# Beginning the moves of a tile's left-over rows from SyncE instead of GpSimd

## The chip, the cores and the metric

The kernel runs on one NeuronCore of a Trainium2 chip. The metric is the device time of one launch in microseconds (us), the median of several runs. Three runs of the kernel before gave 1610.87, 1610.90 and 1611.31 us; the median is 1610.9 us.

## The reference, cut to what matters

Four blocks follow each other over one sequence of 2048 tokens of 512 features: A, B, A, B. Each adds its result to x.

```
x = x + A(layernorm(x));  x = x + B(layernorm(x));  x = x + A(...);  x = x + B(...)

A:  mem = mem0                                # 8 rows
    for s in range(64):                       # 64 segments of 32 tokens, one after the other
        h = concat([mem, xs])                 # 8 + 32 rows
        q, k, v = h@Wq, h@Wk, h@Wv            # 32 heads of 128
        o = softmax(mask(q k^T * scale)) v;  o = o @ Wo
        mem = o[:8];  outs.append(o[8:])      # the memory feeds the next segment

B:  linear attention: kv = sum phi(k) v over all tokens; o = phi(q) kv / (phi(q) z); o @ wo
```

Block A is a recurrence: the first 8 rows of a segment's output are the memory of the next one. Block B needs a sum over all tokens before any of its outputs.

## The kernel before, in words

**Tiles and steps.** The 2048 tokens are 16 tiles of 128 rows. A tile holds four segments, so block A walks through 64 steps s, and tile G = s // 4, g = s % 4. The weights Wq, Wk, Wv and Wo stay in SBUF. Per step TensorE (PE) projects the step's block, forms the scores, multiplies probabilities with v, and projects with Wo (`out_proj`, L1388). VectorE (DVE) and ScalarE (ACT) empty PSUM, and make the softmax.

**Left-over rows.** A step's matmul block has room for 32 rows: 8 of memory and 24 of the segment's 32. The last 8 rows of each of the four segments of a tile ("left") are collected in one block of 32 rows per tile, computed once (`left_block`, L1181), and projected once per tile (`left_rows`, L1445). So rows come back in two ways: 24 rows per step, and 4 times 8 rows per tile.

**Bringing rows home.** `rows_out` (L1434) adds two halves of the projection on DVE (L1437) into a small staging tile `y_sb[:, k]`, and then moves rows by DMA from SBUF to SBUF into `dx_sb`, at the partitions where they belong. k is 0 for a step's 24 rows (two moves of 24x256 elements, 12 KB each), and 1 for the left rows (eight moves of 8x256, 4 KB each; six for the last tile). At the end of a tile one DVE addition (`residual`, L1476) adds `dx_sb` to the tile's x; it waits for all moves of the tile, by the semaphore counts `dy0` and `dy1`. The layer norm of block B (L1099) follows on DVE.

**Who begins the DMAs.** All moves go through `x_move` (L954 and L955), whose default engine is GpSimd (POOL). POOL's queue also holds the stores of x and of the queries to DRAM, the loads of tiles, and in `load_wo_b` (L983) the load of block B's output weight into `MB_sb` (512 KB, a part of the arena), once for each of the two B blocks. SyncE (SP) loads the weights at the start, then begins nothing until the end of the last A block, where `last_rows` (L1625) reloads queries and x with eight loads (L1636), and the results are stored (L1683).

**The order of the work.** It is written out: each operation has a planned time in a table (`PERIOD`, `OWN`), all are sorted by it, and each engine gets its operations in that order. An engine runs its list strictly in order, and each operation waits for the semaphores of what it depends on. So an operation that waits holds back all behind it on its engine. PSUM banks are given out along the same order. The planned times do not depend on the engine that begins a DMA.

On POOL the second weight load stands in the list just ahead of the eight left moves of the tile before the last, and these ahead of two moves of a step's rows. SP's list has, in the kernel before, the loads at the start and then at once the loads of `last_rows`.

Of the kernel before, what the change touches and what calls it, by code (L numbers as in the profile page):

```python
# [596 lines left out]
def c_dve(n, rate=1):  # L597
    return 0.155 + 1.044e-3 * n / rate
# [32 lines left out]
class _Prog:  # L631
# [19 lines left out]
    def add(self, engs, fn, cost, reads=(), writes=(), tiles=(), dsem=None, after=(), lat=0.0, quad=(0, 0), mode=0):  # L651
        nd = _Node()
        nd.lat = lat
        nd.quad = quad
        nd.mode = mode
        nd.key = self.place + (self.count,)
        self.count += 1
        nd.engs = (engs,) if isinstance(engs, str) else tuple(engs)
        nd.cost = cost if isinstance(cost, dict) else {e: cost for e in nd.engs}
        nd.fn = fn  # L660
        nd.sync = set(after)
        nd.order = {self.before[e] for e in nd.engs if e in self.before}
        nd.tiles = tuple(tiles)
        nd.dsem = dsem
        nd.eng = nd.know = None
        nd.sig = False
        nd.val = 0
        nd.waits = []
        nd.idx = len(self.nodes)
        if dsem is not None:  # L670
            self.dma_tot[dsem] = self.dma_tot.get(dsem, 0) + 16
            nd.dval = self.dma_tot[dsem]
        for key in reads:
            st = self.res.setdefault(key, [None, []])
            if st[0] is not None:
                nd.sync.add(st[0])
            st[1].append(nd)
        for key in writes:
            st = self.res.setdefault(key, [None, []])
            if st[0] is not None and st[0] is not nd:  # L680
                nd.sync.add(st[0])
            for r in st[1]:
                if r is not nd:
                    nd.sync.add(r)
            st[0] = nd
            st[1] = []
        for tl in nd.tiles:

            pe = [o for o in tl.ops if o.engs == ("pe",)]
            if nd.engs == ("pe",):  # L690
                if pe:
                    nd.order.add(pe[-1])
                nd.sync.update(tl.ops[tl.ops.index(pe[-1]) + 1:] if pe else [])
            else:
                nd.sync.add(pe[-1])
            tl.ops.append(nd)
        self.nodes.append(nd)
        return nd
# [122 lines left out]
def _build_kernel(nc, A_x, A_mem0, A_Wq, A_Wk, A_Wv, A_Wo, A_seg_len, B_wqkv, B_wo, out):  # L821
# [132 lines left out]
    def x_move(o, i, k, reads, writes, kind, eng="pool", lat=2.0):  # L954
        add(eng, lambda e: e.dma_start(o, i), 0.55 if eng == "pool" else 0.4, reads=reads, writes=writes,  # L955
            dsem="%s%d" % (kind, k), lat=lat + (0.4 if eng == "pool" else 0.0))
# [63 lines left out]
    for j in range(4):  # L1020
        q = slice(32 * j, 32 * j + 32)
        d = j % 2
# [107 lines left out]
    def a_layer(layer):  # L1130
# [303 lines left out]
        def rows_out(w, tl, G, moves):  # L1434

            k = int(w == NW - 1)
            add("dve", lambda v: v.tensor_tensor(y_sb[0:64, k, :], tl.f32()[0:64, 0:256], outW[64:128, w, :].bitcast(F32),  # L1437
                                                 ALU.add),
                c_dve(256), reads=[("outW", w, 0), ("outW", w, 1)], tiles=[tl], writes=[("y", k)], quad=(2, 0))
            for i, (src, dst, n) in enumerate(moves):  # L1440
                for d in range(2):
                    x_move(dx_sb[dst:dst + n, G % 2, 256 * d:256 * d + 256], y_sb[32 * d + src:32 * d + src + n, k, :], k,
                           [("y", k)], [("dx", G % 2, dst, d)], "dy")

        def left_rows(G):  # L1445
            w, tl = out_proj(oTl[:, G % 2, :, :], [[("oTl", G % 2, b)] for b in range(2)], False)
            rows_out(w, tl, G, [(8 * g, 32 * g + 24, 8) for g in range(4 if G < NT - 1 else 3)])

        def residual(G, g, w):

            at(4 * G + g + 1, "res")
            w, tl = w
            xk = ("x", slot(G))
            x = x_sb[:, slot(G), :]
            if G == NT - 1 and g == 3:
                tz = P.tile()

                def pick(pe):
                    for d in range(2):
                        r = pe.matmul(tz.f32()[:, 256 * d:256 * d + 256], selz_sb[:, d, :], outW[:, w, :], start=d == 0,  # L1460
                                      stop=d == 1, skip_group_check=True)
                    return r
                add("pe", pick, 0.42, reads=[("outW", w, 0), ("outW", w, 1), "selz"], tiles=[tz], mode=1)
                add("dve", lambda v: v.tensor_tensor(x, x, tz.f32()[:, :], ALU.add), c_dve(512),
                    reads=[xk], writes=[xk], tiles=[tz])
                return
            rows_out(w, tl, G, [(8, 32 * g, 24)])
            if g == (3 if G < NT - 1 else 2):
                n = 128
                if G < NT - 1:  # L1470
                    left_rows(G)
                else:
                    n = 96
                    at(NSEG - 1, "lr")
                    left_rows(G)
                add("dve", lambda v: v.tensor_tensor(x[0:n, :], x[0:n, :], dx_sb[0:n, G % 2, :], ALU.add), c_dve(512, 2),  # L1476
                    reads=[xk] + [("dx", G % 2, 32 * i + r, d) for i in range(n // 32) for r in (0, 24) for d in range(2)],
                    writes=[xk])
# [26 lines left out]
        for s in range(NSEG):  # L1505
            G, g = divmod(s, 4)
# [233 lines left out]
```

## Time and profile before

| what | value |
|---|---|
| median of 3 runs | 1610.9 us |
| profiled execution, its own time | 1607.17 us |
| profiled execution, span of the profile | 1605.2 us |
| PE busy | 1550.3 us, 97% |
| DVE busy | 1218.7 us, 76% |
| ACT busy | 1101.0 us, 69% |
| POOL busy | 324.9 us, 20% |
| granted TensorE clock, mean | 0.999 |
| moves `dx_sb<-y_sb` begun by POOL | 504, of which 252 of 12 KB and 252 of 4 KB |
| mean time of POOL for one of them | 508 ns |

The profile is one execution, which took 1607.17 us; its span, from the first to the last instruction, is 1605.2 us. The runs without the profiler took 3.7 us more. A row of the timeline gives the start, the duration, the engine and line, the operation, and in brackets the time that the engine stood idle before it and what ended that. The chain of waits follows the last instruction back to what released each step. POOL's time for a DMA is the time to begin it, not the time in which the data move; the landing is told apart.

### The profile page before, as it was taken

How to read it: one execution, taken by the hardware profiler on the slowest of the kernel's cores; microseconds unless marked ns; L12 is line 12 of the kernel's file. 1: busy time of each engine (PE TensorE's matmuls, PEld its weight loads, DVE VectorE, ACT ScalarE, POOL GpSimd, SP SyncE). 2: the span in 40 equal slices, each digit the busy share in tenths (PEclk: the TensorE clock that was granted, in tenths of full speed). 3: DMA queues.
4: the chain of work that ended last, by engine and by line, in shares of the span. 5: the costliest groups of instructions: out<-in, count | busy, mean ns of one | idle time of the engine just before them, and what ended most of it. 6: DMA issues, size and time to landing. Idle time of an engine off the chain costs nothing.

```text
span 1605.2 us, 104159 instructions
## 1 busy us (share of the span) xinstructions
PE 1550.3 (97%) x52121; PEld 880.0 (55%) x43287; DVE 1218.7 (76%) x3865; ACT 1101.0 (69%) x3212; POOL 324.9 (20%) x660
## 2 busy tenths in 40 slices
PE   5899999999999999999999999999999999999997
PEld 1455556555555555555545655556556556555554
DVE  3778888877888887787677777777777777777777
ACT  1566666776666667676566778777777777777665
POOL 2022221122221212222102221222221222221120
PEclk9999999999999999999999999999999999999999
DMA  9300000000000000000000000000000000000013
GB/s 382 104 14 14 10 17 16 17 16 17 13 14 14 17 16 17 17 17 20 22 9 13 17 17 20 20 14 17 21 17 20 20 21 11 21 20 18 21 49 129
DMA packets 35078, 50.96 MB, mean 32 GB/s; under 512 B 13624, under 2 KB 28784, under 8 KB 33104
## 3 DMA queue, kind: packets, MB, share of 16 engines
q0 software_dynamic: 21744, 19.78, 4.3%
q1 hardware_dynamic: 12736, 24.38, 4.1%
q8 instruction: 374, 6.13, 1.6%
q14 instruction: 64, 0.52, 0.1%
q10 hardware_dynamic: 160, 0.14, 0.0%
HBM read 29.63 MB, written 10.49 MB: 25 GB/s over the span
## 4 chain that ended last, share of the span: by engine, by line
PE 88%; DVE 5%; ACT 2%; DMA 2%; issue 1%; POOL 0%; SPq 0%; DVEq 0%; ACTq 0%
PE pb L1159 27%; PE pb L1055 23%; PE pb L1402 18%; PE pb L1067 11%; PE pb L1051 3%; DMA Wv_sb<-in_A_Wv_dram 2%; ACT arena_sb L939 2%; PE pb L1260 1%; PE pb L1426 1%; PE pb L1113 1%; PE pb L1340 1%; DVE st_sb L1099 1%; DVE arena_sb L940 1%; DVE arena_sb L1287 1%; DVE Wq_sb L1681 0%
## 5 line engine op out<-in xcount | busy, mean ns | idle before, releaser
L939 ACT ACTIVATE arena_sb<-pb 128x512 bf16<-128x512 f32 (+5 forms) x1234 | 556.2, 485 | 276.9 <-PE pb L1055 182.2
L955 POOL DMA_DIRECT2D dx_sb<-y_sb x504 | 253.1, 508 | 1055.1 <-DVE y_sb L1437 474.8
L1159 PE MATMUL pb<-Wk_sb,arena_sb 128*32 128x512 bf16 x4096 | 410.3, 380 | 5.4 <-DMA Wq_sb<-in_A_Wq_dram 3.1
L1055 PE MATMUL pb<-Wq_sb,arena_sb 128*32 128x512 bf16 x4096 | 409.6, 379 | 1.2 <-issue 1.2
L940 DVE CAST arena_sb<-pb 128x512 bf16<-128x512 f32 (+3 forms) x510 | 275.7, 544 | 103.4 <-PE pb L1055 66.5
L1402 PE MATMUL pb<-Wo_sb,arena_sb 128*32 128x256 bf16 x10368 | 346.9, 273 | 4.0 <-issue 1.0
L1067 PE MATMUL pb<-arena_sb 128*32 128x128 bf16 (+2 forms) x12528 | 326.8, 216 | 5.0 <-DVE arena_sb L1606 2.0
L1177 DVE STREAM_TRANSPOSE arena_sb<-arena_sb 128x256 f32<-128x256 f32 x640 | 261.5, 431 | 51.2 <-ACT arena_sb L939 44.6
L1067 PEld LDWEIGHTS pb<-arena_sb 128*32 128x32 bf16 x12528 | 227.2, 96 | 130.9 <-issue 39.0
L1159 PE MATMUL pb<-Wv_sb,arena_sb 128*32 128x512 bf16 x3136 | 281.0, 378 | 1.3 <-DMA Wv_sb<-in_A_Wv_dram 0.7
L1402 PEld LDWEIGHTS pb<-Wo_sb,arena_sb 128*32 128x32 bf16 x10368 | 259.1, 97 | 35.8 <-issue 9.2
L1159 PEld LDWEIGHTS pb<-Wk_sb,arena_sb 128*32 128x32 bf16 x4096 | 121.5, 96 | 253.8 <-issue 179.4
L1055 PE MATMUL pb<-Wv_sb,arena_sb 128*32 128x512 bf16 x1984 | 210.3, 378 | 0.0
L939 ACT ACTIVATE arena_sb<-arena_sb 32x256 bf16<-32x256 bf16 (+1 forms) x377 | 143.2, 380 | 14.5 <-DVE arena_sb L1347 4.6
L1159 PEld LDWEIGHTS pb<-Wv_sb,arena_sb 128*32 128x32 bf16 x3136 | 90.0, 96 | 79.2 <-issue 25.1
L939 ACT ACTIVATE outW_sb<-pb 128x128 fp32r<-128x128 f32 x294 | 67.7, 275 | 77.0 <-PE pb L1402 69.1
L1287 DVE TENSOR_TENSOR arena_sb<-arena_sb 128x128 bf16<-128x128 bf16 x504 | 91.8, 216 | 29.5 <-ACT arena_sb L1277 27.7
L1277 ACT ACTIVATE arena_sb<-pb 128x192 bf16<-128x192 f32 (+1 forms) x256 | 85.0, 333 | 41.6 <-PE pb L1260 38.1
L1309 DVE TENSOR_TENSOR arena_sb<-pb,arena_sb 128x128 bf16<-128x128 f32 x252 | 73.0, 290 | 50.4 <-PE pb L1067 24.7
L1159 PE MATMUL pb<-Wq_sb,arena_sb 128*32 128x512 bf16 x1024 | 103.0, 378 | 0.3
L1055 PE MATMUL pb<-Wk_sb,arena_sb 128*32 128x512 bf16 x1024 | 102.3, 378 | 0.0
L940 DVE COPY arena_sb<-arena_sb 32x256 bf16<-32x256 bf16 (+1 forms) x391 | 79.7, 207 | 9.1
(110 smaller groups left out, 1799.4 us busy)
## 6 DMA issues: line engine op xcount, KB each, us to landing
Wk_sb<-in_A_Wk_dram SPq DMA_DIRECT2D x1, 4096.0 KB, 13.7
Wq_sb<-in_A_Wq_dram SPq DMA_DIRECT2D x1, 4096.0 KB, 24.3
Wv_sb<-in_A_Wv_dram SPq DMA_DIRECT2D x1, 4096.0 KB, 33.8
Wo_sb<-in_A_Wo_dram SPq DMA_DIRECT2D x16, 256.0 KB, 7.3
xs_scratch<-x_sb POOLq DMA_DIRECT2D x32, 128.0 KB, 2.7
pq_scratch<-arena_sb POOLq DMA_DIRECT2D x32, 128.0 KB, 3.0
dx_sb<-y_sb POOLq DMA_DIRECT2D x252, 12.0 KB, 1.6
dx_sb<-y_sb POOLq DMA_DIRECT2D x252, 4.0 KB, 1.9
```

Of the source, the lines that this page charges most:

```text
L939: return e.activation(o() if callable(o) else o, i() if callable(i) else i, ACTF.Copy)
L940: return e.tensor_copy(o() if callable(o) else o, i() if callable(i) else i)
L955: add(eng, lambda e: e.dma_start(o, i), 0.55 if eng == "pool" else 0.4, reads=reads, writes=writes, dsem="%s%d" % (kind, k), lat=lat + (0. ...
L1051: return pe.matmul(o, w, x, start=start, stop=stop, skip_group_check=True)
L1055: return pe.add_instruction(mybir.InstMatmult(name=nc.get_next_instruction_name(), engine=mybir.EngineType.PE, ins=[pe.lower_ap(x), pe.low ...
L1067: r = pe.matmul(o[q], w[:, q], x, start=start, stop=stop, skip_group_check=True, tile_position=(0, 32 * j))
L1159: r = pe.matmul(o, blk[:, c, :], w, start=(c == 0), stop=(c == 3), tile_position=(0, 32 * j))
L1177: add("dve", lambda v: v.transpose(dst, src(img[:, k, :].bitcast(F32))), 0.445, reads=[("img", k)], writes=[dkey])
L1277: add("act", lambda a: a.activation(PQ[:, r2, b, 0:nq], tl.f32()[:, 0:nq], ACTF.Exp, scale=SCALE), c_act(nq), tiles=[tl], writes=[("PQ", r ...
L1287: add("dve", lambda v, a=a, p_=p_, w_=w_: v.tensor_tensor(wide(Pm[:, k, a, :]), p_.unsqueeze(2).to_broadcast([128, 4, 4, 8]), w_, ALU.mult ...
L1309: add("dve", lambda v: v.tensor_tensor(oTb[:, s % NO, 16 * b:16 * b + 16, 0:8], pv.f32()[:, 0:128].rearrange("p (n q) -> p n q", q=8), Rm[ ...
L1402: r = pe.matmul(tl.f32()[32 * j:32 * j + 32, 0:256], oT[:, 4 * hh + n, :], Wo_sb[:, 8 * n + hh, 256 * d:256 * d + 256], start=(hh == 0 and ...
```

## The change

The eight moves of a tile's left-over rows (k = 1) are begun by SP. The moves of a step's rows (k = 0), the loads of inputs, x and queries, and the stores stay on POOL. Nothing else is changed: the semaphores are the same, and the order of operations on PE, DVE and ACT is the same. SP's list gets 252 moves: 246 stand ahead of the first load of `last_rows`, and the six of the last tile stand between the second and the third of these loads. POOL's list loses the same 252.

```diff
             for i, (src, dst, n) in enumerate(moves):
                 for d in range(2):
                     x_move(dx_sb[dst:dst + n, G % 2, 256 * d:256 * d + 256], y_sb[32 * d + src:32 * d + src + n, k, :], k,
-                           [("y", k)], [("dx", G % 2, dst, d)], "dy")
+                           [("y", k)], [("dx", G % 2, dst, d)], "dy", ("pool", "sp")[k])
```

## The prediction

> **What bounds the kernel now.** I read the page first: its first part (busy time) and fourth part (the chain that ended last).
>
> ```profile
> PE 1550.3 (97%) x52121; PEld 880.0 (55%) x43287; DVE 1218.7 (76%) x3865; ACT 1101.0 (69%) x3212; POOL 324.9 (20%) x660
> ...
> PE 88%; DVE 5%; ACT 2%; DMA 2%; issue 1%; POOL 0%; SPq 0%; DVEq 0%; ACTq 0%
> ```
>
> TensorE is the bound and POOL has 80% of its time free. So a shorter queue on POOL is worth nothing on average; what counts is the few places where POOL is late. The same follows from the group of the moves: POOL stood idle 1055.1 us ahead of them.
>
> Next, all instructions that touch dx_sb, and who waited for these moves:
>
> ```profile
> L955 POOL DMA_DIRECT2D dx_sb<-y_sb x504: 497/507/537, 62.5 to 1566.5; - x168
> L1476 DVE TENSOR_TENSOR x_sb<-x_sb,dx_sb x32: 412/421/427, 99.4 to 1569.1; 128x512 bf16<-128x512 bf16 x30, 96x512 bf16<-96x512 bf16 x2
> ...
>   DVE x_sb L1476: 2.7, 3
> ```
>
> Of 32 tile ends only 3 waited visibly, 2.7 us together. By DVE's timeline these are 1.81 us at 1489.96, 0.52 at 754.82 and 0.34 at 1060.63. The chain of waits around the longest:
>
> ```profile
> 1482.32 0.28 issue
> 1482.61 0.77 POOL arena_sb L984
> 1483.38 4.49 POOL dx_sb L955 x9
> 1487.87 2.00 DMA dx_sb<-y_sb
> ```
>
> Here POOL sets the end of the program. Its weight load (L984) waits for PE until 1482.61, and eight left moves, whose data DVE had finished at 1480.07, stand behind it, and two row moves behind those. What that costs PE is seen by comparing this tile with the one before. Columns: start, duration, engine, line, and in brackets the idle time ahead. First DVE, then PE, then the first projection matmul of the next step as a landmark.
>
> ```profile
> 1440.74 0.42 DVE L1476 TENSOR_TENSOR x_sb<-x_sb,dx_sb 128x512 bf16<-128x512 bf16 x1
> ...
> 1489.96 0.43 DVE L1476 TENSOR_TENSOR x_sb<-x_sb,dx_sb 128x512 bf16<-128x512 bf16 x1 [1.81 <-DMA dx_sb<-y_sb]
> ```
>
> ```profile
> 1442.21 0.24 PE L1067 MATMUL pb<-arena_sb,one_sb 128*32 128x128 bf16 x4 [0.63 <-DVE arena_sb L1287]
> ...
> 1446.54 0.40 PE L1159 MATMUL pb<-Wk_sb,arena_sb 128*32 128x512 bf16 x4
> ...
> 1491.43 0.24 PE L1067 MATMUL pb<-arena_sb,one_sb 128*32 128x128 bf16 x4 [2.46 <-DVE arena_sb L1287]
> ...
> 1497.13 0.39 PE L1159 MATMUL pb<-Wk_sb,arena_sb 128*32 128x512 bf16 x4
> ```
>
> PE's gap is 0.63 us in a normal tile of the second A block and 2.46 here, 1.83 more. After it the same work takes 1497.13 - 1491.43 = 5.70 us instead of 1446.54 - 1442.21 = 4.33, 1.37 more, because the granted clock is low (the column after the busy times, 1.00 against 0.57):
>
> ```profile
> 1442.20:1446.20 4.00, 3.86 (x184) 3.47 (x180) 2.64 (x12) 3.76 (x16) 0.00 (x0) 1.00 0.12 39
> 1491.40:1495.40 4.00, 3.97 (x116) 3.14 (x112) 2.47 (x11) 2.59 (x10) 0.00 (x0) 0.57 0.10 35
> ```
>
> Together this stall costs 3.20 us. PE is busy without a hole after it, so a microsecond saved here reaches the end.
>
> **What is removed from POOL.** Eight issues of about 0.50 us (508 ns is the group's mean), 4.0 us a tile. In 30 tiles they lie beside PE's work and DVE finds the rows landed, so removing them there gives nothing. At 1482.61 they are on the path. Without them POOL is free at 1483.38; the row data are ready at 1484.26 (DVE L1437, 1483.84 + 0.42); POOL begins about 0.3 us after such an end (first left move 1432.76 after 1432.47), so the row moves begin at 1484.55 and 1485.06. The weight load ahead of them in the same queue landed at 1487.1, and left moves that POOL began at 1484.9 and 1485.4 behind it landed at 1487.24 and 1487.45, so I take 1487.4 for the rows. DVE ended the work before L1476 at 1488.16. The whole 1.81 us goes, with 0.7 us in hand, and PE's gap falls back to 0.63 us.
>
> **What that gap does to the clock** is where a page and the row are to be weighed. The row: gaps of 0.63 us, and one of 1.06 at 1062.10, kept the clock at full speed; the one of 2.46 was followed by 3.4 us at half. The Trainium skill, "TensorE: Matmul & The Clock Gate", section "What's actually happening", says that the monitor's window of 3413 ns runs freely, so that when a gap trips it depends on the phase. By the row the change earns 1.83 + 1.37 = 3.20 us; by the rule the runs without the profiler may never have had the 1.37, and it earns 1.83. The three runs lie within 0.44 us, so they all had it or all did not. I take the row, and keep the other as a case.
>
> **The two small stalls.** At 1060.63 PE's gap was 1.06 instead of 0.63, so 0.43 us; at 754.82 the first transpose came 3.38 us after DVE was ready, 3.10 in its neighbours, so 0.28 us. At 1060.63 the left moves had landed in time; late was a row move that POOL began 2.05 us after it was free and its data there, while a 16 KB packet of the instruction queue ran. POOL shows such pauses of 1.5 to 2.05 us a few times. The change moves them elsewhere: POOL has 365 DMAs instead of 617, so some five pauses, and 2 of the 12 DMAs of a tile are the pair that counts. A pause there costs about 0.9 us (rows ready 1056.39, needed 1060.29, 3.9 us; 0.3 + 0.5 + 2.1 are used, 1.0 is spare). Between 0 and 1.8 us in all; I take 0.4 (half a hit), against 0.71 won. Sum: 3.20 + 0.71 - 0.4 = 3.5 us.
>
> **What is added to SP.** The trace has no SP move of 8 partitions. The near rows: SP's output stores at 332 ns median, up to 1045, and the one DMA of 8 partitions begun by a like queue, ACT's first, at 609 ns.
>
> ```profile
> L955 SPq DMA_DIRECT2D out_dram<-Wq_sb x15: 332/332/1045, 1588.6 to 1603.0; - x15
> ...
> L965 ACTq DMA_DIRECT2D arena_sb<-in_A_mem_dram x1: 609/609/609, 0.8 to 0.8; - x1
> ```
>
> The bounds are 0.33 and 0.65 us with a step between, I take 0.5. SP waits for DVE's y of the left rows; only further left moves are behind it, until the end. From the left y to the moment DVE needs it, the profile has 7.8 us in the first A block (185.20 to 192.98) and 8.0 to 8.3 in the second. Needed are 0.3 + 7 x 0.5 + 1.9 to land (the median of the 4 KB moves) = 5.7 us; with 0.65 it is 6.75. Hidden both ways, with 1.0 us in hand at worst. In the stalled tile the left moves would then be begun from 1480.4 to 1484.4 and land by 1486.8, before 1488.16 too.
>
> **The end of the last A block.** SP's first two reloads (L1636) begin at 1558.58 and 1559.00 and landed at 1563.26 and 1564.71. The six last left moves follow at 1562.5 (y at 1562.20), 6 x 0.5 = 3 us, so the third reload, which began at 1559.55, slips to 1565.5, and lands about 1571. The fourth waits for a store until 1570.89 anyway. Their readers are after 1578. The left moves may wait behind the reloads' data, and the row moves (landed 1569.02 now) beside the third; DVE needs them for L1476 at 1569.11, but idles 1.32 us after it for PE. Up to 1.3 us later costs nothing; I put 0, with a bound of +0.7.
>
> **Rivals.**
> 1. *Partial or no gain.* The same skill's page "DMA: Bandwidth & Descriptors", section "Issuing engines are not separate DMA queues", says that all queues end on the same 16 engines and that another issuer saves only the issue time, usually small. By it the rows would still queue behind the weight load, and the time stays at 1610.9; by the row, 4.49 us of issue stand on the chain and not data. Between them: without the clock's share 1610.9 - 1.83 - 0.3 = 1608.8. For it: the landing beside 512 KB of other data. Against it: the 0.7 us in hand.
> 2. *Slower: SP is slower per move than thought.* With c per move the left rows land 0.3 + 7c + 1.9 us after y. From c = 0.80 in the first and 0.83 in the second A block every tile end waits. At c = 0.9 this is 0.7 x 15 + 0.5 x 15 = 18 us, 1629; at 1.04, the longest store on SP, 1.7 x 15 + 1.5 x 15 = 48 us, 1659. For it: that 1.04 row, and 609 for 8 partitions. Against it: 332 is the median for sixteen times the rows.
> 3. *The change does not do what it says*: excluded, SP's list holds the moves.
>
> **How the numbers follow.** The profiled time is 1607.17 and its span 1605.2; the sum is made in that span, to 1601.7, and I carry the difference to the median: 1610.9 - 3.5 = 1607.4 us. A measurement of this kernel can tell about 0.2%, 3.2 us, from no change: faster is below 1607.7, slower above 1614.1. The likeliest case, both parts of the stall gone, has 0.62 and its own range 1606.3 to 1608.3; I put 0.52 of it below 1607.7. Rival 1 has 0.22, all within 0.2%, to 1611. Rival 2 has 0.16. So faster 0.52, same 0.32, slower 0.16. The range 1605.9 to 1612.5 leaves out nearly all of rival 2 and little else; its lower end is 3.2 + 0.71 + 1.1 for tile ends that the profile shows without a stall by less than 0.1 us.
>
> **What would show it.** Right: in the tile near 1486 DVE L1476 without a wait, PE's gap at 0.63, and no stretch of low clock between the start and the end; POOL's moves 252, SP's 252 at about 0.5 us or less. Wrong: DVE L1476 waiting in every tile (rival 2), a wait that stays near 1489 (rival 1), or new waits behind POOL's pauses.

## The result, and the profile after

The changed kernel takes 1607.6 us (median of 15 runs, 1603.70 to 1610.39), the kernel before 1610.9 us (median of 15 runs beside them, 1608.41 to 1614.12). The ratio is 0.9975, with a 95% interval of 0.9967 to 0.9983. Of 1610.9 us that is 4.0 us less, between 2.7 and 5.3; the two medians differ by 3.3. The forecast was 1607.4.

The profiled execution took 1609.4 us, its span is 1607.4. It is one of the longer ones of the changed kernel, and longer than the profile of before (1605.2). Executions of one kernel differ by some 6 us, so the two spans can't be set against each other; what can be compared is the same place in several profiles, and medians.

One sentence of the description of the kernel is to be corrected: the second weight load stands ahead of the left moves of the fourteenth of the sixteen tiles (G = 13) of the second A block, the last but two, and not of the tile before the last. It is called "the tile" below.

The page of the changed kernel, its first and fourth parts:

```profile
PE 1544.6 (96%) x52074; PEld 883.0 (55%) x43287; DVE 1218.8 (76%) x3865; ACT 1100.9 (68%) x3212; POOL 199.0 (12%) x408
...
PE 88%; DVE 4%; DMA 3%; ACT 2%; issue 2%; SPq 0%; DVEq 0%; POOL 0%
```

POOL lost 252 of its 660 instructions and 126 us, and the bound is the same: PE sets 88% of the chain, as before. All instructions that touch dx_sb, with their least, median and largest time in ns, and who waited:

```profile
L955 POOL DMA_DIRECT2D dx_sb<-y_sb x252: 505/505/524, 63.1 to 1568.1; - x126
L955 SPq DMA_DIRECT2D dx_sb<-y_sb x252: 624/625/1585, 91.8 to 1567.4; - x126
L1476 DVE TENSOR_TENSOR x_sb<-x_sb,dx_sb x32: 415/419/425, 100.0 to 1571.9; 128x512 bf16<-128x512 bf16 x30, 96x512 bf16<-96x512 bf16 x2
...
  DVE x_sb L1476: 3.9, 3
```

A move of 4 KB takes SP 625 ns, where a move of 4 or 12 KB takes POOL some 505. The waits of L1476 are as many as before, 3, and in sum they are longer, 3.9 us against 2.7. DVE's timeline says where they are:

```profile
787.05 0.42 DVE L1476 TENSOR_TENSOR x_sb<-x_sb,dx_sb 96x512 bf16<-96x512 bf16 x1 [2.03 <-DMA dx_sb<-y_sb]
...
1493.13 0.42 DVE L1476 TENSOR_TENSOR x_sb<-x_sb,dx_sb 128x512 bf16<-128x512 bf16 x1 [0.75 <-DMA dx_sb<-y_sb]
...
1571.92 0.42 DVE L1476 TENSOR_TENSOR x_sb<-x_sb,dx_sb 96x512 bf16<-96x512 bf16 x1 [1.07 <-DMA dx_sb<-y_sb]
```

Two of them are at the end of an A block (96 rows), where the profile of before had none; the two small ones at 754.82 and 1060.63 are gone; the one in the tile has fallen from 1.81 to 0.75 us, but has not gone. What happened there on SP and POOL (start, duration, engine, line, idle time ahead):

```profile
1484.12 5.29 SPq L955 DMA_DIRECT2D dx_sb<-y_sb  x8
```

```profile
1486.83 0.77 POOL L984 DMA_DIRECT2D arena_sb<-in_B_wo_dram  x1 [8.15 <-PE pb L1067]
1488.76 1.01 POOL L955 DMA_DIRECT2D dx_sb<-y_sb  x2 [1.16 <-DVE arena_sb L940]
```

SP begins the left moves while POOL still waits for its weight load, and POOL is free 1.16 us before the row moves can begin. The chain of waits through the same place shows what is late now:

```profile
1488.05 0.42 DVE y_sb L1437
...
1488.76 0.50 POOL dx_sb L955
1489.26 3.77 DMA dx_sb<-y_sb
...
1493.13 0.44 DVE x_sb L1476
```

In the profile of before, POOL stood 4.49 us on this chain; now it stands 0.50, and the landing of one row move stands 3.77 instead of 2.00. PE's gap, and the granted clock after it (last column but two):

```profile
1494.60 0.24 PE L1067 MATMUL pb<-arena_sb,one_sb 128*32 128x128 bf16 x4 [1.27 <-DVE arena_sb L1287]
```

```profile
1494.60:1498.60 4.00, 4.00 (x196) 3.55 (x188) 2.83 (x13) 3.62 (x14) 0.00 (x0) 1.00 0.12 39
```

The gap is 1.27 us where 2.46 were and 0.63 were expected, and the clock stays at 1.00 where it fell to 0.57.

### The profile page after: what moved, and what is told of

Its sections match the earlier page's. It is cut to its first block, busy times and chain, and to the rows that moved or that the text cites. A ratio compares the mean times of both kernels' runs of the same rounds, so it can differ in the third digit from the quotient of the medians.

```text
span 1607.4 us, 104112 instructions
## 1 busy us (share of the span) xinstructions
PE 1544.6 (96%) x52074; PEld 883.0 (55%) x43287; DVE 1218.8 (76%) x3865; ACT 1100.9 (68%) x3212; POOL 199.0 (12%) x408
## 4 chain that ended last, share of the span: by engine, by line
PE 88%; DVE 4%; DMA 3%; ACT 2%; issue 2%; SPq 0%; DVEq 0%; POOL 0%
PE pb L1159 27%; PE pb L1055 23%; PE pb L1402 18%; PE pb L1067 11%; PE pb L1051 3%; DMA Wv_sb<-in_A_Wv_dram 2%; ACT arena_sb L939 2%; PE pb L1260 1%; PE pb L1426 1%; PE pb L1113 1%; PE pb L1340 1%; DVE st_sb L1099 1%; DVE arena_sb L1287 1%; DVE arena_sb L940 1%; DMA dx_sb<-y_sb 0%
## 5 line engine op out<-in xcount | busy, mean ns | idle before, releaser
L955 POOL DMA_DIRECT2D dx_sb<-y_sb x252 | 127.2, 508 | 1170.9 <-DVE arena_sb L940 598.6
L1437 DVE TENSOR_TENSOR y_sb<-pb,outW_sb 64x256 bf16<-64x256 f32 x158 | 65.9, 417 | 27.4 <-ACT outW_sb L939 23.2
```

## The experiments

The theory on trial: the gain is the stalled tile (3.20 us of the sum) and little else, because the left moves' issue time stood in POOL's list there. Against it stand three others: that the tile is a small part and the gain comes from the other 31 tile ends; that it is another queue's order and not the engine that counts; and, for the far side, that SP has a price per move from which every tile end waits. All kernels compute the whole reference.

### The tile alone

```diff
-                           [("y", k)], [("dx", G % 2, dst, d)], "dy")
+                           [("y", k)], [("dx", G % 2, dst, d)], "dys" if k and (layer, G) == (1, 13) else "dy", "sp" if k and (layer, G) == (1, 13) else "pool")
```

Only the eight left moves of the tile are begun by SP, with a semaphore of their own.

> Only the eight left moves of the tile that stands behind the second weight load (the fourteenth tile of the second A block) are begun by SP, under a semaphore of their own; all others stay on POOL. Theory H (the gain is the head of POOL's queue in that one tile): 1607.4 to 1608.6 us where before has 1610.9, so -2.3 to -3.5; DVE's wait for L1476 near 1490 falls from 1.8 to below 0.8 us. Theory W (POOL is relieved in all tiles): one tile of 32 gives about 0.1 us, 1610.8, and the wait near 1490 is only a symptom.

Measured: 1608.86 us against 1611.69, ratio 0.9981 (0.9965 to 0.9996). A second time, on another chip:

> One tile's left moves on SP once more, for a narrower interval. Two profiles and the trace of four stalled tiles give 2.4 us for that tile (100.8 against 98.3 us from the tile end before it to the one after), so 0.9985; the first measurement had 0.9981.

Measured: 1605.6 against 1607.64, 0.9988 (0.9978 to 0.9998). The two together, weighted by their intervals, give 0.9986 with 0.0008 to either side: 2.3 us, between 1.0 and 3.6.

### All but the tile

The same edit with `!=` in the place of `==`: SP begins all left moves but the eight of the tile.

> The left moves of all tiles but that one are begun by SP; that one's stay on POOL behind the weight load. Theory H: no gain, 1610 to 1613 us; the wait of 1.8 us near 1490 is there as before, and single tile ends wait about 1 to 2 us where a move's packet meets an instruction packet on its DMA engine. Theory W: 1607.6, as the whole change.

Measured: 1609.4 against 1611.69, 0.9981 (0.9968 to 0.9993). The second time:

> All tiles but that one once more, for a narrower interval. If the rest of the gain sits in the other tiles (POOL's pauses, which fall from seven to one), 0.9985 to 0.9991; by theory H alone 1.000. The first measurement had 0.9981.

Measured: 1606.48 against 1607.64, 0.9997 (0.9986 to 1.0008). Together 0.9990 with 0.0008 to either side: 1.6 us, between 0.3 and 2.9. The product with the tile's 0.9986 is 0.9976, which is the whole change. So the tile is the larger part by its middle value, and the other tile ends have a share; the sum on record gave them 0.3 us, the lower end of what was measured. The intervals are too wide to say how the two stand to each other.

What that share is, the profiles say better than the times. In seven profiles the left moves and the row moves of the other tiles are in one list, POOL's (the kernel before in two profiles, the tile alone in two, and three further ones below); in six they are in two lists (the changed kernel in two profiles, all but the tile in two, and two below). PE's first matmul after a tile end, near 384 and near 1069 in the kernel before, run once more, and then the one near 1067 in the changed kernel:

```profile
384.51 0.24 PE L1067 MATMUL pb<-arena_sb,one_sb 128*32 128x128 bf16 x4 [1.71 <-DVE arena_sb L1287]
...
1069.01 0.24 PE L1067 MATMUL pb<-arena_sb,one_sb 128*32 128x128 bf16 x4 [1.08 <-DVE arena_sb L1287]
```

```profile
1066.93 0.24 PE L1067 MATMUL pb<-arena_sb,one_sb 128*32 128x128 bf16 x4 [0.63 <-DVE arena_sb L1287]
```

At the later tile end the gap is 1.01 to 1.08 us in all seven profiles with one list, and 0.62 or 0.63 in all six with two. The first of the three lines belongs to a tile end that the profile of before shows as harmless (L1476 waits 0.11 us at 379.2): in three of the seven profiles L1476 waits 1.80 to 2.31 us there, and PE has a gap of 1.20 to 1.71 us; in the six with two lists it never waits. In the other profiles PE has no gap over 0.15 us there, so over the seven the stall is (1.71 + 1.60 + 1.20) / 7 = 0.64 us on average. Two things meet in it: in all seven POOL begins the last row move some 1.5 us after its data are there (one of its pauses, see below), and in the three late ones a 16 KB packet of the instruction queue then runs, and the move lands 1.01 to 1.08 us after that packet's end.

### The order of POOL's list instead of another engine

```diff
-    (1, 64, 'ldwo'): '1515835',
+    (1, 64, 'ldwo'): '1523000',
```

The kernel before with the planned time of the second weight load put behind the tile's moves. Nothing is on SP.

> The kernel before with one planned time changed: the second weight load stands on POOL behind that tile's left and row moves instead of ahead of them. No move goes to SP. Theory H: the whole gain or slightly more, 1606.9 to 1608.0 us, no wait for L1476 near 1490 and PE's gap there 0.6 us. Theory W, and the theory that SP's own way of beginning a DMA is what helps: 1610.9.

Measured: 1609.74 against 1611.69, 0.9987 (0.9975 to 0.9999), as much as the tile alone with SP (0.9986). POOL's timeline in the tile, and PE's:

```profile
1485.37 3.95 POOL L955 DMA_DIRECT2D dx_sb<-y_sb  x8 [5.70 <-DVE y_sb L1437]
1489.61 1.03 POOL L955 DMA_DIRECT2D dx_sb<-y_sb  x2 [0.29 <-DVE arena_sb L940]
1490.63 0.78 POOL L984 DMA_DIRECT2D arena_sb<-in_B_wo_dram  x1
```

```profile
1494.60 0.24 PE L1067 MATMUL pb<-arena_sb,one_sb 128*32 128x128 bf16 x4 [0.63 <-DVE arena_sb L1287]
```

The left moves begin with their data, and the rows 0.29 us after theirs, because nothing ahead of them waits. PE's gap is the normal 0.63. What cost time in the tile was the weight load that waits for PE at the head of a list in order: taking the moves out of that list, or the load out of their way, are two cures of one thing. The other tile ends keep their stalls here (L1476 waits 2.21 us at 382.52, 0.16 at 756.38 and 0.34 at 1064.26), which fits a gain smaller than that of the full change, though the two intervals overlap.

### The kernel before once more

No edit.

> The kernel before once more, for a second profile and for what two equal kernels differ by: ratio 1.000 within 0.001; the wait of 1.8 us near 1490 is there again by theory H. Whether the clock falls after it a second time is open[...].

Measured: 1611.28 against 1611.69, 0.9994 (0.9980 to 1.0008). Its profiled execution took 1616.49 us. The spread of one kernel in one session is as large as twice the effect; a single profile can't carry a verdict on it.

### The same wait, made longer

```diff
+                    parts = 4 if k and (layer, G) == (1, 13) else 1
+                    for c in range(parts):
+                        m = 256 // parts
...
+                        x_move(dx_sb[dst:dst + n, G % 2, 256 * d + m * c:256 * d + m * c + m],
...
```

In the kernel before, the tile's eight left moves are cut in 32 moves of 8x64, all on POOL: 24 issues more and not a byte more.

> The kernel before, but in that one tile (the fourteenth of the second A block) each of the eight left moves is cut into four of a quarter of the columns: 32 moves on POOL, the same bytes. Theory H (time to begin them at the head of POOL's queue sets the end): 24 more issues of 0.50 us are 12 us, so DVE waits about 13.8 us at L1476 instead of 1.8 and the time is 1622 to 1625 against 1611. The rule that the data on the DMA engines are what counts, and theory W: no change, 1611.

Measured: 1624.4 against 1612.44, 12.0 us more, 1.0082 (1.0068 to 1.0096). POOL's timeline and DVE's:

```profile
1487.06 0.77 POOL L984 DMA_DIRECT2D arena_sb<-in_B_wo_dram  x1 [7.94 <-PE pb L1067]
1487.82 16.80 POOL L955 DMA_DIRECT2D dx_sb<-y_sb  x34
```

```profile
1505.77 0.42 DVE L1481 TENSOR_TENSOR x_sb<-x_sb,dx_sb 128x512 bf16<-128x512 bf16 x1 [13.15 <-DMA dx_sb<-y_sb]
```

24 issues at 16.80 / 34 = 0.494 us are 11.9 us, and the medians differ by 12.0 (by the ratio's interval 11.0 to 15.5). Within that width, issue time on that spot is paid one to one, though not a byte more is moved.

### What POOL's pauses hang on

The prediction put POOL's pauses of 1.5 to 2.05 us down to its instruction packets. In the trace of before there are seven, of 0.82 to 2.05 us, and they come at the DMAs of POOL with the numbers 131, 205, 281, 357, 400, 471 and 551. If they hang on the place in POOL's instructions, 40 more instructions must move them.

```diff
+    for _ in range(40):
+        add("pool", lambda p: p.memset(pad_sb[:, :], 0.0), 0.1, writes=["pad"])
...
```

> The kernel before with 40 small memsets of an unused tile on POOL after its setup, in time in which it waits. Theory P (POOL's pauses of 1.5 to 2 us at its DMAs number 131, 205, 281, 400, 471 and 551 belong to places in its instruction stream): the pauses come at other DMAs, earlier by a common shift, and the waits for L1476 near 383 (2.3 and 2.2 us in two of the profiles) and near 1062 (0.34) go or move to other tiles; that near 1490 stays at 1.5 to 1.8. Against P (the pauses belong to the work or to the time): they stay at the same DMAs. In time 1608 to 1612, not to be told from before.

Measured: 1613.03 against 1612.44, 1.0001 (0.9991 to 1.0011). The pauses stayed at the same seven DMAs. So they don't hang on the place in POOL's instructions, but go with the place in its list of DMAs. Nor do they need a packet of the instruction queue: in the profile of before none runs during four of the seven (131, 205, 281 and 357). The changed kernel, with 365 DMAs on POOL, shows one pause, 2.66 us at DMA 131, which is in another tile than before and delays nothing.

### Both cures at once

```diff
-    (1, 64, 'ldwo'): '1515835',
+    (1, 64, 'ldwo'): '1523000',
...
-                           [("y", k)], [("dx", G % 2, dst, d)], "dy")
+                           [("y", k)], [("dx", G % 2, dst, d)], "dys" if k and G < NT - 1 else "dy", "sp" if k and G < NT - 1 else "pool")
```

The left moves of the last tile of each A block stay on POOL, all others go to SP, and the weight load is behind the tile.

> Left moves on SP in all tiles but the last of each A block, with a semaphore of their own, and the second weight load behind the row moves of its tile. Theories H and P together: no wait near 1490 and one pause of POOL instead of seven, 1605.5 to 1607.5 against 1611, 1 us or less under the change alone. If the change's gain came from somewhere else, the load's place adds nothing: 1607.6 to 1608.

Measured: 1608.26 against 1612.44, 0.9975 (0.9967 to 0.9984). The changed kernel beside it, without an edit:

> The changed kernel once more, beside the others on one chip, for a second profile: ratio 0.9975 within 0.0015, 1606 to 1609; the wait near 1490 is 0 to 1 us, POOL pauses once, near its DMA 131; single tile ends wait where an instruction packet holds one engine of a move.

Measured: 1608.41 against 1612.44, 0.9977 (0.9968 to 0.9986). The second cure adds nothing that can be measured to the first. In the changed kernel's second profile L1476 in the tile doesn't wait, and PE's gap is 0.62; in the first it was 1.27. What is left of the tile's stall under the change comes and goes.

### The price per move on SP

```diff
+                    for c in range(2 if k else 1):
+                        m = 128 if k else 256
...
+                        x_move(dx_sb[dst:dst + n, G % 2, 256 * d + m * c:256 * d + m * c + m],
...
```

The changed kernel with each left move cut in two: sixteen moves of 2 KB per tile on SP.

> The changed kernel with each left move cut into two of half the columns: 16 moves a tile on SP, the same bytes. The rival of the prediction (SP's time per move decides once it exceeds what the tile leaves free) with c = 0.67 us between begins: the last lands 15 x 0.67 + 1.7 = 11.8 us after y, DVE wants it after 7.8 to 8.0, so every tile end of 30 waits about 3.9 us, 117 us, and where the clock falls up to 1.5 us more each: 1720 to 1770. If the times between begins shrink with the size of a move (half the bytes), the waits stay under 1 us and the time under 1640.

Measured: 1763.6 against 1607.64, 156 us more, 1.0982 (1.0956 to 1.1008). The view of dx_sb, and the chain through one tile end:

```profile
L955 SPq DMA_DIRECT2D dx_sb<-y_sb x504: 624/624/1342, 91.2 to 1723.9; - x168
...
  DMA dx_sb<-y_sb: 123.1, 32
```

```profile
195.20 0.42 DVE y_sb L1437
...
204.35 0.62 SPq L955
205.02 0.62 SPq L955
205.69 0.62 SPq L955
206.35 1.67 DMA dx_sb<-y_sb
208.05 0.44 DVE x_sb L1480
```

A move of half the size takes SP the same 624 ns, and begins 0.667 us after the one before it. Sixteen of them end far behind the 7.9 us that DVE gives them (y at 195.62, L1480 wanted at 208.05 - 4.57 = 203.48), so all 32 tile ends wait, 123.1 us in sum. On PE, gaps of over 0.15 us are 155.9 us in sum where the changed kernel has 51.9, so 104 more, and PE is busy for 121.5 us at a granted clock of 0.5 where it was 6.8, which costs some 57 us more; the two make 161 us, near the 156 measured. The mean clock falls to 0.959. This is the mechanism of rival 2: the change is a gain only as long as eight moves fit under that cover.

### The rows on SP instead

```diff
-    (1, 64, 'ldwo'): '1515835',
+    (1, 64, 'ldwo'): '1523000',
...
-                           [("y", k)], [("dx", G % 2, dst, d)], "dy")
+                           [("y", k)], [("dx", G % 2, dst, d)], "dy", ("sp", "pool")[k])
```

SP begins the moves of a step's rows, POOL keeps the left moves, and the weight load is behind the tile.

> The other way round, with the second weight load behind its tile's moves: the two row moves of each step on SP, the left moves and all else on POOL. A row pair on SP needs 0.03 + 0.67 + 1.7 = 2.4 us of the 3.9 it has, where POOL needed 2.9 and had pauses; so no tile end waits but for an instruction packet: 1605.5 to 1608 against 1611, no better than the two measures together (0.9975). If SP is no better a place for rows, 1609 to 1611.

Measured: 1604.78 against 1607.64, 0.9982 (0.9970 to 0.9995). The mirror image gains as well. The weight load's new place alone gave 0.9987 (0.9975 to 0.9999), and the times can't tell the two apart; the profile can: L1476 doesn't wait near 380 nor near 1060, where PE's gap is 0.63. So at these ends what helps is that the left moves and the row moves are in different lists, whichever engine has which.

```profile
L955 SPq DMA_DIRECT2D dx_sb<-y_sb x252: 713/714/1512, 62.1 to 1564.3; - x126
```

SP needs 714 ns for a move of 24 partitions and 12 KB, 625 for 8 partitions and 4 KB. None of these versions is faster than the changed kernel by more than the intervals.

## Why the prediction was right, point by point

**The tile.** The place and the mechanism were right: the tile alone on SP gains 2.3 us (1.0 to 3.6), the load out of the way gains the same, and a longer queue there is paid in full. The size, 3.20 us, lies within what the times allow, but by the profiles it was too large. Twelve profiles show the tile ("span" is the time from the tile end before it to the tile end after it; in the last three rows the load is behind the moves):

| kernel | L1476 waits | PE's gap | clock after | span |
|---|---|---|---|---|
| before | 1.81 | 2.46 | low | 101.0 |
| before once more | 1.45 | 2.17 | low | 101.2 |
| all but the tile | 1.31 | 2.02 | low | 101.5 |
| all but the tile, 2nd | 1.58 | 2.30 | full | 99.2 |
| POOL with 40 memsets | 1.29 | 2.01 | full | 99.4 |
| changed | 0.75 | 1.27 | full | 98.6 |
| changed once more | 0 | 0.62 | full | 97.9 |
| the tile alone | 0.35 | 1.07 | full | 98.8 |
| the tile alone, 2nd | 0.15 | 0.87 | full | 98.1 |
| load later | 0 | 0.63 | full | 97.8 |
| both | 0 | 0.62 | full | 98.4 |
| rows on SP | 0.51 | 1.23 | full | 98.2 |

With the left moves behind the load (first five rows) the span is 100.5 us on average, with them on SP (next four) 98.4. That is 2.1 us in place of 3.20, and the difference is in both of its terms:

- *PE's gap falls back to 0.63 us, with 0.7 us in hand.* It falls to 0.96 us on average, from 2.19. The step that failed is the landing of the rows at 1487.4. The rows begin 0.29 us after their data, as said (1488.05 + 0.42, then 1488.76). Then the estimate had 2.85 us from the first begin to the last landing (1484.55 to 1487.4); in the changed kernel it was 4.27 (1488.76 to 1493.03), where 3.62 were to be had. The late one is the second row move: the estimate had 2.34 us for it (1485.06 to 1487.4), and in the four profiles with the moves on SP it took 2.91 to 3.77. One thing stands beside it each time: a 16 KB packet of the instruction queue runs there, from 1490.77 to 1491.85 in the changed kernel, and the move lands 1.18 to 1.25 us after the end of that packet in all four. The weight load's data had landed before the move did (1491.36 against 1493.03 here). That the packet held the move up is read from these times, and was not put to a trial.
- *The clock, 1.37 us.* The clock fell after three of the five gaps of 2.0 to 2.5 us, and not after a gap of 2.30 while it did after one of 2.02. Here the Trainium skill ("TensorE: Matmul & The Clock Gate", section "What's actually happening"), with its window that runs freely, is the better guide to a single execution: the length of a gap doesn't decide alone. The row was the better guide to the price: the three spans with a low clock are 101.2 on average, the two without 99.3, 1.9 us apart, so 3 in 5 of that is 1.2 us. The argument that the three runs, within 0.44 us, all had the fall or all did not doesn't hold: fifteen runs of the kernel before lie 5.7 us apart. Averages of the granted clock over the whole span, which every execution reports, say the same with more executions (those of the kernel before stood beside all the experiments):

| kernel | executions | mean granted clock |
|---|---|---|
| before | 105 | 0.99776 |
| all but the tile | 24 | 0.99783 |
| the tile alone | 24 | 0.99863 |
| changed | 26 | 0.99915 |

A difference of 0.001 is 1.6 us of full clock. The tile alone brings 0.00087, 1.4 us with about 1.0 to either side; all but the tile brings 0.1 with as much to either side; the whole change brings 0.00139, 2.2 us with about 0.6 to either side. This speaks against rival 1's case "without the clock", 1608.8 us: about half of what the change brings goes with the clock. That the whole brings 2.2 and the tile 1.4 may be chance or another gap that no longer trips; this stays open.

**The two small stalls.** At 1060.63 the term of 0.43 us was right: 1.01 to 1.08 against 0.62 or 0.63, in every profile. At the tile end near 755 L1476 waits 0.16 to 0.52 us in five of the seven profiles with one list and in none of the six with two, but the 0.28 us that PE was said to lose by it can't be told from the spread. What failed is the term "-0.4" for POOL's pauses: "some five pauses" were one, it lies where nothing waits, and the instruction packet beside the one pause that was looked at tells nothing, since none runs during four of the seven. And a third stall was missed, the tile end near 380, since the profile of before happened to show 0.11 us there: 0.64 us on average. So 0.31 us on record (0.71 - 0.4) are 0.43 + 0.64 + up to 0.28, some 1.2 us; the runs say 1.6 (0.3 to 2.9).

**The sum.** 2.1 for the tile and some 1.2 for the others are 3.3 us, the sum on record was 3.5. That the total was so near was luck: two errors went against each other, by 1.1 and by 0.9 us.

**SP's price per move.** Taken as 0.5 us, bounded by 0.33 and 0.65; it is 0.625 to begin one and 0.667 from one begin to the next, just outside. The near row was that of 8 partitions on ACT's queue (609 ns), not the stores of 128 partitions (332). The cover held as told: 7 x 0.667 + 1.67 to land, and 0.06 to 0.3 ahead, are 6.4 to 6.6 us of 7.8, with 1.2 in hand instead of the worst case's 1.0. Rival 2 was on the right scale and is shown by the sixteen moves; its point of 0.80 us was 0.13 away.

**Rival 1, by the skill.** That another issuer saves only the issue time (the Trainium skill, "DMA: Bandwidth & Descriptors", section "Issuing engines are not separate DMA queues") is true of one move (0.5 us to begin, 1.9 to land) and misleads here, where nine begins stood in a row: 4.49 us on the chain, and 24 issues more cost 12.0 us. That another issuer doesn't free a move of the traffic of others shows in the traces as well: with the left moves on SP the second row move still took 2.91 to 3.77 us to land.

**The end of the last A block.** Put at 0 with a bound of +0.7. L1476 waits 1.07 us at 1571.92, inside the 1.3 us that it had. From the tile end before it to the end of the span it is 63.98 and 63.19 us in the two profiles of the changed kernel, and 63.42 and 64.39 in those of the kernel before. Costed at nothing, and rightly, as far as that spread can tell.

**What would show it.** "L1476 without a wait" and "gap at 0.63" came true in one of two profiles of the changed kernel. "No stretch of low clock between the start and the end" came true in the second only: in the first, one follows the wait of 2.03 us at 787.05. That wait, 1.2 to 2.0 us, is in most of the kernels, the one before among them (1.28 at 788.60 in its second profile), so it isn't the change's doing.

## What to carry to other kernels

A queue that is idle four fifths of the time can still set the end of the program, where one instruction that waits for the bound engine stands ahead of others whose data are ready; read the few places, not the share, and see whether the order of the list cures it as well as another engine would. Small DMAs are priced by the piece: count them, multiply by the issue time of the engine that begins them, and compare with the time until their reader comes. Where an effect is as small as the spread of single executions, one profile gives the mechanism and not the size: it showed a clock drop that comes three times in five, and hid a stall that comes three times in seven.

## What the hardware showed that was not expected

- SP needs more time for a small move than POOL: 625 ns for 8 partitions and 714 for 24, POOL 505 to 508 for either, while SP's stores of 128 partitions take 332. Half the bytes (2 KB) take the same 624.
- In the kernel before, a move of 4 or 12 KB lands 1.9 us after its begin (median; nine in ten within 2.6), but it takes 3 to 4 us in several places where a packet of the instruction queue (16 KB, 0.9 to 1.7 us long) runs beside it. In the changed kernel the move begun at 783.26 landed at 786.95: seven of its eight packets of 512 bytes went by 784.62, an instruction packet ran from 784.90 to 785.77, and the eighth went at 785.76. A packet stands in the same way beside the move that was late at 1493.03, and beside those of three other profiles that were late near 380. It was seen in each of these, and was not put to a trial.
- Begins on SP stretch as well: 15 of the 252 took over 0.7 us, up to 1.585, and an instruction packet runs beside 13 of them. The longest, 780.30 to 781.88, lies over an instruction packet from 780.22 to 781.48.
- POOL pauses 0.8 to 2.7 us at fixed numbers in its list of DMAs, the same seven in the seven profiles with one list; 40 more instructions ahead of them moved none. The reason was not found.
